# A table that fixes the order of every engine's queue in a fused attention and FFN kernel

## The chip, the cores and the metric

The kernel runs on one core of a Trainium2 chip. The metric is the device time of one execution in microseconds (us), the median of several. The core has TensorE (PE, matrix products and transposes), VectorE (DVE), ScalarE (ACT), GpSimd (POOL) and SyncE (SP, which here only issues transfers). Each takes its instructions in the order of its own queue.

## The reference

Attention over 8 batches, 8 heads, 576 positions and 64 dimensions, in two versions that are added: one over q, k and v averaged over groups of four positions and then repeated four times, one local, in which a position sees only those less than four away. The sum is laid out as 4608 tokens of 512 and goes through a two-layer FFN.

```python
factor = 4; scale = 1.0 / np.sqrt(D)
q_d = q.reshape(B, H, Sd, factor, D).mean(axis=3)      # k_d, v_d in the same way
out_up = np.repeat(sm_attn(q_d, k_d, v_d), factor, axis=2)
mask = np.abs(pos[:, None] - pos[None, :]) < factor
scores = np.where(mask, scale * np.matmul(q, k.transpose(0, 1, 3, 2)), -1000000000.0)
attn_out = out_up + np.matmul(softmax(scores), v)
x = attn_out.transpose(0, 2, 1, 3).reshape(B * S, H * D)      # 4608 x 512
h = x @ w_in                                                   # 512 x 2048
g = np.maximum(h, 0.0) + alpha * np.minimum(h, 0.0)
out = g @ w_out                                                # 2048 x 512
```

## The kernel before

Products run in fp32r with each operand split into a high and a low part (xh and xl, wih and wil, woh and wol, gh and gl), three products for one. The FFN is cut into 18 chunks of 256 tokens and each chunk into 8 steps of 256 hidden columns, 144 steps in all. Step number st does this:

- `hidden` (L784): 24 matmuls of 128x256 on TensorE into the PSUM tile h (two buffers, h0, h1, ...);
- `slopes` (L799, L801, L803): ScalarE makes t and sh, or scales h, from alpha;
- `larger` (L811 on DVE, or L76, a helper for additions on POOL): joins the two into t. POOL does it in 30 of the first 32 steps, DVE later;
- `split`: ScalarE casts t to gh (L816), POOL takes gl = t - gh (L73);
- `product` (L845): 12 matmuls of 128x512 into the chunk's two output tiles, o0_0 and o0_1 for chunk 0. After 8 steps ScalarE copies them to sg (L851) and SP stores them.

The weights come as 64-bit numbers and are decoded in the kernel by `make`, in 8 blocks for each matrix (raw0_0 to raw0_7 for w_in, raw1_0 to raw1_7 for w_out; the last ones in halves such as raw1_60 and raw1_61): ScalarE's magnitude (L197), DVE's L201, L202, L206 and L207, ScalarE's cast of the high part (L212 for wih, L216 for woh), DVE's low part (L220 for wil, L224 for wol).

The first batch of the attention is done by `first_batch`, four head pairs one after another (names with f: fs scores, fp and fpt probabilities, fpv their product with v, fxs, rest). Its last DVE lines are L534 (the sum of local and averaged attention, fxs) and L541 (xl = fxs - xh). Since x spans all heads, the first step can end its sums only with the fourth pair's xl0.

Later batches are done beside the FFN. `down` does the averaged attention of one batch and one head pair (qkT2_2 is batch 2, pair 2): loads ld (L247, three buffers), POOL's sums over four positions (L76, ld folded, then s2q, s2k, s2v), TensorE's transposes qkT (L265), ScalarE's copies qd and kd (L270, L273), scores s (L278), probabilities dp, their transposes pT (L302), ScalarE's copy th (L306), and pv (L312). `local` does the local attention in units on DVE, with some sums on POOL, and TensorE's transposes xp (L682) give the x tiles. qkT, s, pT, pv and xp share one PSUM tag of two buffers.

The order of the work is set in two ways. All these pieces stand in a list of events with planned times. Events before the time LISTED = 14 are handed to the tile scheduler, which orders each engine's queue by its own estimates, with some hints: `tc.issue_after` holds a load behind the load of a weight block (the table BEHIND), the first late magnitude behind a slope, and one local product behind the end of another unit. Events from 14 on are kept in the order of the list by `tc.manual_schedule()`. The last lines of the function are these (L1002 to L1011):

```python
    for t, _, f, args in events:
        if t < LISTED:
            f(*args)
    with tc.manual_schedule():
        for t, _, f, args in events:
            if t >= LISTED:
                f(*args)
```

Of the kernel before, what the change touches and what calls it, by code (L numbers as in the profile page):

```python
# [47 lines left out]
BEHIND = {(1, 0): ((0, 2), (0, 2)), (1, 1): ((1, 4), (0, 5)), (1, 2): ((1, 5), (1, 5))}  # L48
FAR = {3: 2, 4: 2, 5: 2, 6: 2}
LISTED = 14  # L50
JOINS = (0.04, 0.06)


@with_exitstack
def tile_attention_moe(ctx: ExitStack, tc: tile.TileContext, q, k, v, w_in, w_out, alpha, out):
# [24 lines left out]

# [43 lines left out]

# [7 lines left out]

    raws, turns, issued, sloped = {}, [0, 0], {}, {}
    weights_temp = []

    def load_raw(which, fp, blocks=(0, 1)):
        raw = raws.setdefault((which, fp), {})
        if fp < NP - 2:
            raw[None] = one.tile([128, 1024, 2], I32, tag=f"slot{turns[0] % 3}", name=f"raw{which}_{fp}")
# [2 lines left out]
        src = (w_in, w_out)[which].bitcast(I32)  # L150
        for c in blocks:
            if fp < NP - 2:
                dst = raw[None][:, 512 * c:512 * c + 512]
            elif fp == NP - 2:
                dst = raw[c] = late.tile([128, 512, 2], I32, tag="prod", name=f"raw{which}_{fp}{c}", bufs=PB)
            else:
                dst = raw[c] = late.tile([128, 512, 2], I32, tag=f"x{'hl'[c]}", name=f"raw{which}_{fp}{c}")
            if which == 0:
                issued[which, fp] = nc.sync.dma_start(dst.rearrange("p (k a) b -> p k (a b)", k=2),
                                  bass.AP(src.tensor, 256 * c * 2 * DF + 512 * fp, [[2 * DF, 128], [256 * DF, 2], [1, 512]]))  # L160
            else:
                row = 256 * fp + 128 * c
                issued[which, fp] = nc.sync.dma_start(dst.rearrange("p a b -> p (a b)"), src[row:row + 128, :])
# [8 lines left out]

    def make(which, fp, c=None):
# [12 lines left out]
        def magnitude():  # L188
# [7 lines left out]
            with tc.issue_after(sloped[0].ins) if (which, fp) == (0, N_EARLY) else nullcontext():  # L196
                nc.scalar.activation(f32(st["t"]), f32(st["raw"][:, :, :, 1]), AF.Abs)  # L197
# [31 lines left out]

# [137 lines left out]

# [8 lines left out]

# [6 lines left out]

# [202 lines left out]


    def local(u, t0, t1):
# [183 lines left out]

# [45 lines left out]

# [37 lines left out]

# [15 lines left out]


# [103 lines left out]

# [59 lines left out]
```

## Time and profile before

| | |
|---|---|
| median of 3 runs | 983.32 us (983.08 to 987.91) |
| profiled execution | 982.8 us |
| its span in the trace | 981.0 us |
| mean granted TensorE clock | 0.976 of full speed |
| busy: PE, DVE, ACT, POOL | 942.9, 819.5, 555.3, 527.6 us |

The profile is of one execution. Its span runs from the first to the last instruction; the execution's own time is 1.8 us longer. Busy time is the time in which an engine has an instruction in work; idle time of an engine is put down in the trace to what released it (in square brackets behind an instruction: how long the engine stood idle before it, and which instruction of which engine ended that). A full granted clock of TensorE is 2.4 GHz, half of it 1.2 GHz. Line numbers are those of the kernel before.

### The profile page before, as it was taken

What the parts mean: (1) busy time and instruction counts of PE and PEld (TensorE: products, weight loads), DVE (VectorE), ACT (ScalarE), POOL (GpSimd) and SP (SyncE); (2) the same over time, 40 slices, a digit from 0 to 9 for tenths busy, and PEclk for the clock granted to TensorE, in tenths of its full rate; (3) what the DMA queues carried; (4) which work ended last, traced back from release to release, by engine and by line L of the source; (5) the groups of instructions that cost most, each with busy time, mean ns of one, the idle gap of its engine ahead of it and who ended that gap; (6) DMA issues with size and microseconds to landing.
All of it is one profiled execution on the core that took longest, in us unless ns stands there. A gap on an engine that the chain in (4) does not pass through costs nothing.

```text
span 981.0 us, 17943 instructions
## 1 busy us (share of the span) xinstructions
PE 942.9 (96%) x6402; PEld 842.0 (86%) x6402; DVE 819.5 (84%) x1318; ACT 555.3 (57%) x1483; POOL 527.6 (54%) x642
## 2 busy tenths in 40 slices
PE   5878999999999999999999999999999999999998
PEld 4757887987888888989988899898899989999997
DVE  7999978888879999998889899899898889997111
ACT  4767776544645655556554655565556664544442
POOL 2055877787887546555537365555466633323221
PEclk9956999999999999999999999999999999999999
DMA  8946723132333322422322423332333321310000
GB/s 200 232 146 208 254 90 107 61 114 85 111 101 116 114 76 88 139 80 83 119 78 86 127 86 93 108 98 68 105 112 103 110 63 46 97 34 22 1 22 22
DMA packets 63197, 98.28 MB, mean 100 GB/s; under 512 B 23556, under 2 KB 28932, under 8 KB 63108
## 3 DMA queue, kind: packets, MB, share of 16 engines
q1 hardware_dynamic: 62916, 96.88, 32.8%
q8 instruction: 50, 0.82, 0.3%
q10 hardware_dynamic: 192, 0.26, 0.1%
q14 instruction: 39, 0.32, 0.1%
HBM read 87.67 MB, written 9.44 MB: 99 GB/s over the span
## 4 chain that ended last, share of the span: by engine, by line
PE 59%; DVE 11%; POOL 4%; ACT 3%; issue 2%; DMA 1%; SPq 0%; DVEq 0%; POOLq 0%
PE o L845 28%; PE h L784 27%; DVE lb L673 3%; DVE pv L670 2%; DVE qk L614 1%; PE s L278 1%; PE pv L312 1%; DVE t L811 1%; DVE ls L618 1%; PE xp L682 1%; POOL t L76 1%; PE pT L302 1%; DVE xf L698 1%; ACT t L799 1%; POOL gl L73 1%
## 5 line engine op out<-in xcount | busy, mean ns | idle before, releaser
L73 POOL TENSOR_TENSOR gl<-t,gh 128x512 fp32r<-128x512 f32 x144 | 186.3, 1294 | 323.4 <-ACT gh L816 303.3
L799 ACT ACTIVATE t<-h,slope 128x256 f32<-128x256 f32 x288 | 136.3, 473 | 128.8 <-PE h L784 105.7
L845 PE MATMUL o<-woh,gh 128*128 128x512 f32 x576 | 192.8, 405 | 2.5 <-ACT gh L816 1.1
L784 PE MATMUL h<-xh,wih 128*128 128x256 f32 x1152 | 188.0, 285 | 2.6 <-ACT sh L801 1.9
L845 PE MATMUL o<-wol,gh 128*128 128x512 f32 x576 | 185.7, 393 | 0.0
L845 PE MATMUL o<-woh,gl 128*128 128x512 f32 x576 | 185.4, 393 | 0.0
L784 PE MATMUL h<-xh,wil 128*128 128x256 f32 x1152 | 180.7, 279 | 0.0
L784 PE MATMUL h<-xl,wih 128*128 128x256 f32 x1152 | 180.5, 279 | 0.0
L784 PEld LDWEIGHTS h<-xh,wih 128*128 128x128 f32 x1152 | 162.8, 190 | 13.0 <-ACT sh L801 2.6
L816 ACT CAST gh<-t 128x512 fp32r<-128x512 f32 x144 | 89.5, 622 | 140.3 <-DVE t L811 81.6
L76 POOL TENSOR_TENSOR ld<-ld 72x256 f32<-72x256 f32 x168 | 131.9, 787 | 67.4 <-DMA ld<-in_q 64.8
L784 PEld LDWEIGHTS h<-xh,wil 128*128 128x128 f32 x1152 | 155.3, 190 | 0.3
L784 PEld LDWEIGHTS h<-xl,wih 128*128 128x128 f32 x1152 | 154.6, 190 | 0.1
L811 DVE TENSOR_TENSOR t<-h,t 128x512 f32<-128x512 f32 x114 | 78.3, 687 | 88.2 <-ACT h L803 87.8
L618 DVE TENSOR_REDUCE ls<-qk 128x12 f32<-128x768 f32 (+1 forms) x126 | 136.2, 1083 | 3.1
L845 PEld LDWEIGHTS o<-woh,gl 128*128 128x128 f32 x576 | 108.0, 188 | 24.0
L845 PEld LDWEIGHTS o<-wol,gh 128*128 128x128 f32 x576 | 108.0, 188 | 23.1 <-DVE temp L207 0.2
L673 DVE TENSOR_TENSOR lb<-lb,pv 128x384 f32<-128x384 f32 x202 | 114.0, 564 | 5.9
L845 PEld LDWEIGHTS o<-woh,gh 128*128 128x128 f32 x576 | 99.1, 188 | 18.9 <-issue 2.6
L803 ACT ACTIVATE h<-h,sign 128x256 f32<-128x256 f32 x228 | 100.2, 439 | 0.0
L670 DVE TENSOR_TENSOR pv<-v,lb 128x1152 f32<-128x1152 f32 x84 | 93.6, 1115 | 2.7
L614 DVE TENSOR_TENSOR qk<-k,qp 128x768 f32<-128x768 f32 (+1 forms) x78 | 84.0, 1078 | 4.6 <-ACT qp L607 4.6
(151 smaller groups left out, 1185.7 us busy)
## 6 DMA issues: line engine op xcount, KB each, us to landing
k<-in_k SPq DMA_DIRECT2D x41, 384.0 KB
v<-in_v SPq DMA_DIRECT2D x41, 384.0 KB
out<-sg SPq DMA_DIRECT2D x140, 64.0 KB
raw<-in_moe_w_in SPq DMA_DIRECT2D x16, 512.0 KB
raw<-in_moe_w_out SPq DMA_DIRECT2D x16, 512.0 KB
ld<-in_q SPq DMA_DIRECT2D x56, 144.0 KB
ld<-in_k SPq DMA_DIRECT2D x56, 144.0 KB
ld<-in_v SPq DMA_DIRECT2D x56, 144.0 KB
```

The source lines that it names most:

```text
L73: nc.gpsimd.tensor_tensor(o, a, b, op=ALU.subtract)
L76: nc.gpsimd.tensor_tensor(o, a, b, op=ALU.add)
L614: nc.vector.tensor_tensor(st["pr"][:, :nd], window(tiles[u, "k"], half, d0, nd), st["qp", half].unsqueeze(1).to_broadcast([128, nd, 2, 192 ...
L618: nc.vector.tensor_reduce(out=st["s"][:, half, d0:d0 + nd, :].rearrange("p a b -> p (a b)"), in_=st["pr"][:, :nd].rearrange("p a h (t d) - ...
L670: nc.vector.tensor_tensor(st["pr"][:, :nd], window4(tiles[u, "v"], half, d0, nd), prob(half, d0, nd), op=ALU.mult)
L673: nc.vector.tensor_tensor(st["acc"], st["acc"], st["pr"][:, i], op=ALU.add)
L784: nc.tensor.matmul(ph[:, j], w[:, m, 128 * o:128 * o + 128], x[:, m, :], start=(i == 0), stop=(i == 11))
L799: nc.scalar.activation(t[:, j], hs[st][:, j], AF.Copy, scale=slope[:, f:f + 1])
L803: nc.scalar.activation(other[:, j], hs[st][:, j], AF.Copy, scale=sign[:, f:f + 1])
L811: nc.vector.tensor_tensor(gs[st], hs.pop(st), gs[st], op=ALU.max)
L816: nc.scalar.copy(gh, t)
L845: nc.tensor.matmul(outs[c][m], g[:, j, 128 * m:128 * m + 128], wo[w][n][:, o, :], start=(f == 0 and i == 0), stop=(f == NF - 1 and i == 2))
```

## The change

A table ORDERS holds for each of PE, DVE, Activation, Pool and SP the names of the tiles in the order in which they are to be written; `h1*8` is eight operations on tile h1, `temp@1` the second of the operations on temp that are still open. After all operations have been emitted, a loop goes through the instructions, looks up the next one of each named tile, and ties each operation of an engine behind the one ahead of it on the same engine. `manual_schedule`, BEHIND, the calls of `issue_after` and what they needed go. The numbers of instructions stay.

```diff
-BEHIND = {(1, 0): ((0, 2), (0, 2)), (1, 1): ((1, 4), (0, 5)), (1, 2): ((1, 5), (1, 5))}
+ORDERS = {
+    "PE": """
...
+    o2_0 o2_1 o2_0 o2_1 o2_0 o2_1 o2_0 o2_1 o2_0 o2_1 pT2_1_0*3 pT2_1_1*3 h23*24 qkT2_2*4 xp5_0*3 o2_0 o2_1 o2_0
...
-            with tc.issue_after(sloped[0].ins) if (which, fp) == (0, N_EARLY) else nullcontext():
-                nc.scalar.activation(f32(st["t"]), f32(st["raw"][:, :, :, 1]), AF.Abs)
+            nc.scalar.activation(f32(st["t"]), f32(st["raw"][:, :, :, 1]), AF.Abs)
...
-            behind = BEHIND.get((b, hp))
-            with tc.issue_after(issued[behind[i // 3]].ins) if behind else nullcontext():
-                nc.sync.dma_start(st[i].rearrange("p g f d -> p (g f d)"),
-                                  bass.AP(src.tensor, (b * H + 2 * hp + i % 2) * HEAD, [[512, 72], [1, 512]]))
+            nc.sync.dma_start(st[i].rearrange("p g f d -> p (g f d)"),
+                              bass.AP(src.tensor, (b * H + 2 * hp + i % 2) * HEAD, [[512, 72], [1, 512]]))
...
-            with tc.issue_after(ended[3].ins) if (u, half, d0) == (4, 0, 0) else nullcontext():
-                nc.vector.tensor_tensor(st["pr"][:, :nd], window(tiles[u, "k"], half, d0, nd),
-                                        st["qp", half].unsqueeze(1).to_broadcast([128, nd, 2, 192]), op=ALU.mult)
+            nc.vector.tensor_tensor(st["pr"][:, :nd], window(tiles[u, "k"], half, d0, nd),
+                                    st["qp", half].unsqueeze(1).to_broadcast([128, nd, 2, 192]), op=ALU.mult)
...
-    with tc.manual_schedule():
-        for t, _, f, args in events:
-            if t >= LISTED:
-                f(*args)
+    for t, _, f, args in events:
+        if t >= LISTED:
+            f(*args)
+
+    queues = {e: [] for e in ORDERS}
+    for i in nc.cur_bb.bb.instructions:
+        e = str(i.engine).split(".")[-1]
+        ap = getattr(i.outs[0], "bass_ap", None) if len(i.outs) else None
+        if e in ORDERS and ap is not None:
+            queues[e].append((re.sub(r"_\d+$", "", ap.tensor.name), i))
+    for e, listed in ORDERS.items():
+        by_name, line = {}, []
+        for name, i in queues[e]:
+            by_name.setdefault(name, []).append(i)
+        for name, _, n in (x.partition("*") for x in listed.split()):
+            name, _, k = name.partition("@")
+            line += [by_name[name].pop(int(k or 0)) for _ in range(int(n or 1))]
+        placed = {i.name for i in line}
+        line += [i for _, i in queues[e] if i.name not in placed]
+        for i, j in zip(line, line[1:]):
+            tc.add_manual_dep(j, i.name, mybir.DependencyInfo(mybir.DependencyClass.NoSync, mybir.DependencyReason.DATA),
+                              reason="order")
```

What moves, engine by engine: SP's queue is the same before and after. PE's differs in its first 445 us or so, DVE's, ACT's and POOL's about as far; behind that all queues are as they were. Three places follow, before and then after. The line numbers behind the change are those of the changed program (L534, L571 and L1045 there are L265, L302 and L784 before; L363 and L360 are L76 and L73; L807, L800, L493, L474, L475, L479 and L480 are L541, L534, L220, L201, L202, L206 and L207).

The first place is DVE, where the first batch's fourth head pair meets the decode of the fourth weight blocks. DVE before:

```order
L202 TENSOR_SCALAR temp_208<-temp_208 128x1024
L220 TENSOR_TENSOR wil1_855<-temp_208,wih1_854 128x4x256
L534 TENSOR_TENSOR fxs30_796<-fpv30_787,fod3_785 128x256
L206 SCALAR_TENSOR_TENSOR temp_208<-raw1_3_882,temp_208 128x1024
L282 TENSOR_REDUCE dnb1_0_1082<-s1_0_1067 96x3
L534 TENSOR_TENSOR rest_106<-fpv38_813,fod3_785 128x64
L201 TENSOR_SCALAR temp_208<-temp_208 128x1024
L541 TENSOR_TENSOR xl0_108<-fxs30_796,xh0_107 128x256
```

DVE with the change:

```order
L800 TENSOR_TENSOR fxs30_796<-fpv30_787,fod3_785 128x256
L480 SCALAR_TENSOR_TENSOR temp_208<-raw0_3_872,temp_208 128x1024
L474 TENSOR_SCALAR temp_208<-temp_208 128x1024
L475 TENSOR_SCALAR temp_208<-temp_208 128x1024
L807 TENSOR_TENSOR xl0_108<-fxs30_796,xh0_107 128x256
L493 TENSOR_TENSOR wil1_855<-temp_208,wih1_854 128x4x256
L479 SCALAR_TENSOR_TENSOR temp_208<-raw1_3_882,temp_208 128x1024
L800 TENSOR_TENSOR rest_106<-fpv38_813,fod3_785 128x64
L480 SCALAR_TENSOR_TENSOR temp_208<-raw1_3_882,temp_208 128x1024
L474 TENSOR_SCALAR temp_208<-temp_208 128x1024
L800 TENSOR_TENSOR fxs34_809<-fpv34_800,fod3_785 128x256
L551 TENSOR_REDUCE dnb1_0_1082<-s1_0_1067 96x3
```

fxs30 went ahead of the last decode operations of block raw0_3, and xl0 ahead of wil1, of raw1_3's first operations, of rest and of dnb1_0.

The second place is PE near step 23, where qkT2_2 is the transpose for batch 2, pair 2, and o2_0 and o2_1 belong to chunk 2. PE before:

```order
L845 MATMUL o2_0_2492<-wol2_915,gh20_2704 128x512
L845 MATMUL o2_1_2493<-wol2_915,gh20_2704 128x512
L845 MATMUL o2_0_2492<-woh2_914,gl20_2705 128x512
L845 MATMUL o2_1_2493<-woh2_914,gl20_2705 128x512
L265 MATMUL qkT2_2_2877<-ident_75,s2q2_2_2609 128x72 x2
L265 MATMUL qkT2_2_2877<-ident_75,s2k2_2_2691 128x72 x2
L784 MATMUL h23_2884<-xh2_1758,wih3_1283 128x256 x4
L784 MATMUL h23_2884<-xh2_1758,wil3_1284 128x256 x4
L784 MATMUL h23_2884<-xl2_1759,wih3_1283 128x256 x4
```

PE with the change:

```order
L1105 MATMUL o2_0_2490<-woh2_914,gl20_2703 128x512
L1105 MATMUL o2_1_2491<-woh2_914,gl20_2703 128x512
L571 MATMUL pT2_1_0_2834<-ident_75,dp2_1_2693 72x96 x3
L571 MATMUL pT2_1_1_2838<-ident_75,dp2_1_2693 72x96 x3
L1045 MATMUL h23_2882<-xh2_1758,wih3_1283 128x256 x4
L1045 MATMUL h23_2882<-xh2_1758,wil3_1284 128x256 x4
L1045 MATMUL h23_2882<-xl2_1759,wih3_1283 128x256 x4
L1045 MATMUL h23_2882<-xh2_1758,wih3_1283 128x256 x4
L1045 MATMUL h23_2882<-xh2_1758,wil3_1284 128x256 x4
L1045 MATMUL h23_2882<-xl2_1759,wih3_1283 128x256 x4
L534 MATMUL qkT2_2_2875<-ident_75,s2q2_2_2607 128x72 x2
L534 MATMUL qkT2_2_2875<-ident_75,s2k2_2_2689 128x72 x2
```

Before, the twelve o matmuls of step 20 stood between pT2_1_1 and qkT2_2 (the last four are shown), and h23 behind qkT2_2; now the twelve stand ahead of pT2_1_0, and all 24 matmuls of h23 stand between pT2_1_1 and qkT2_2.

The third place is POOL in the second batch's second head pair (ld1_1_4 and ld1_1_5 are its tiles of v, s2v1_1 their sums; t3 belongs to step 3). POOL before:

```order
L76 TENSOR_TENSOR ld1_1_4_1157<-ld1_1_4_1157 72x2x128
L76 TENSOR_TENSOR s2k1_1_1194<-ld1_1_3_1125 72x2x64
L76 TENSOR_TENSOR ld1_1_5_1201<-ld1_1_5_1201 72x2x128
L76 TENSOR_TENSOR t0_1019<-sh0_1020,t0_1019 128x512
L76 TENSOR_TENSOR s2v1_1_1248<-ld1_1_4_1157 72x2x64
L76 TENSOR_TENSOR s2v1_1_1248<-ld1_1_5_1201 72x2x64
L73 TENSOR_TENSOR gl0_1033<-t0_1019,gh0_1032 128x512
L76 TENSOR_TENSOR t1_1073<-sh1_1074,t1_1073 128x512
```

POOL with the change:

```order
L363 TENSOR_TENSOR t1_1073<-sh1_1074,t1_1073 128x512
L360 TENSOR_TENSOR gl1_1087<-t1_1073,gh1_1086 128x512
L363 TENSOR_TENSOR t2_1133<-sh2_1134,t2_1133 128x512
L363 TENSOR_TENSOR ld1_1_5_1201<-ld1_1_5_1201 72x2x128
L360 TENSOR_TENSOR gl2_1163<-t2_1133,gh2_1162 128x512
L363 TENSOR_TENSOR t3_1218<-sh3_1219,t3_1218 128x512
L363 TENSOR_TENSOR ld1_1_4_1157<-ld1_1_4_1157 72x2x128
L363 TENSOR_TENSOR s2v1_1_1248<-ld1_1_4_1157 72x2x64
L363 TENSOR_TENSOR s2v1_1_1248<-ld1_1_5_1201 72x2x64
```

The sums of v for that pair went from between t0 and gl0 to behind t3.

## Rows read from the trace of the kernel before

**Rows 1.** The page, busy time of each engine: us, share of the span, instructions.

```profile
PE 942.9 (96%) x6402; PEld 842.0 (86%) x6402; DVE 819.5 (84%) x1318; ACT 555.3 (57%) x1483; POOL 527.6 (54%) x642
```

**Rows 2.** Stretches: us, busy PE, PEld, DVE, ACT, POOL, then PEclk, DMA share, GB/s.

```profile
50.00:75.00 25.00, 19.27 (x122) 14.80 (x122) 24.97 (x43) 15.66 (x41) 13.05 (x12) 0.50 0.38 135
75.00:100.00 25.00, 20.14 (x139) 17.38 (x138) 24.63 (x31) 18.11 (x43) 15.26 (x12) 0.68 0.70 232
100.00:125.00 25.00, 25.00 (x161) 22.35 (x160) 22.82 (x30) 18.34 (x48) 22.09 (x26) 1.00 0.69 232
225.00:250.00 25.00, 22.70 (x143) 19.89 (x142) 21.66 (x42) 11.12 (x35) 19.79 (x26) 0.93 0.26 80
330.00:900.00 570.00, 569.05 (x3894) 513.07 (x3893) 521.56 (x841) 319.62 (x867) 296.64 (x368) 1.00 0.29 89
```

**Rows 3.** Timeline of DVE, 80 to 100 us: start us, us, engine, line, operation.

```profile
80.70 1.22 DVE L220 TENSOR_TENSOR wil<-temp,wih 128x1024 fp32r<-128x1024 f32 x1
...
81.83 0.42 DVE L534 TENSOR_TENSOR fxs<-fpv,fod 128x256 f32<-128x256 f32 x1
...
84.55 0.41 DVE L541 TENSOR_TENSOR xl<-fxs,xh 128x256 fp32r<-128x256 f32 x1
...
99.66 4.40 DVE L220 TENSOR_TENSOR wil<-temp,wih 128x1024 fp32r<-128x1024 f32 x1
```

**Rows 4.** Waits of DVE in 0 to 130 us: total us, times, longest.

```profile
DVE fv L493 <- DMA fv<-in_v: 3.9, 2, 2.1
```

**Rows 5.** Timeline of PE, 50 to 160 us, as rows 3, idle time before in brackets.

```profile
72.23 2.13 PE L515 MATMUL fpt<-ident,fp 128*70 128x128 f32 x9 [3.22 <-DVE fp L510]
...
92.69 0.73 PE L784 MATMUL h<-xh,wih 128*128 128x256 f32 x4 [1.87 <-ACT sh L801]
...
99.36 0.51 PE L845 MATMUL o<-woh,gh 128*128 128x512 f32 x1 [1.05 <-ACT gh L816]
...
126.79 0.51 PE L784 MATMUL h<-xh,wih 128*128 128x256 f32 x2 [0.70 <-ACT wih L212]
...
149.13 0.74 PE L845 MATMUL o<-woh,gh 128*128 128x512 f32 x2 [0.67 <-ACT woh L216]
...
157.71 0.51 PE L845 MATMUL o<-woh,gh 128*128 128x512 f32 x1 [0.73 <-ACT sg L851]
```

**Rows 6.** Timeline of PE, 225 to 330 us, the three longest idle times.

```profile
231.03 0.50 PE L265 MATMUL qkT<-ident,s2q 72*128 72x72 f32 x2 [2.24 <-ACT th L306]
...
259.75 0.34 PE L265 MATMUL qkT<-ident,s2q 72*128 72x72 f32 x2 [1.42 <-ACT th L306]
...
289.72 0.65 PE L682 MATMUL xp<-ident,x 128*128 128x128 f32 x4 [0.93 <-ACT kd L273]
```

**Rows 7.** The chain of waits, 226 to 265 us: start us, us, what.

```profile
227.19 1.28 POOL t L76
...
230.66 0.32 ACT th L306
...
231.77 3.97 PE h L784 x24
...
248.75 2.07 DMA ld<-in_v
...
260.22 2.79 PE h L784 x24
```

**Rows 8.** Timeline of POOL, 98 to 114 us, as rows 3.

```profile
98.62 1.85 POOL L76 TENSOR_TENSOR s2v<-ld 72x128 f32<-72x128 f32 x2
...
113.21 1.32 POOL L76 TENSOR_TENSOR t<-sh,t 128x512 f32<-128x512 f32 x1
```

**Rows 9.** Timeline of SP, the transfers' queue, 80 to 160 us, as rows 3.

```profile
118.16 0.90 SPq L163 DMA_DIRECT2D raw<-in_moe_w_out  x2
...
124.09 1.68 SPq L163 DMA_DIRECT2D raw<-in_moe_w_out  x2
```

**Rows 10.** Timeline of ACT, 135 to 144 us, as rows 3.

```profile
135.18 0.66 ACT L197 ACTIVATE temp<-raw 128x512 f32<-128x512 f32 x1
```

More of the change, by code (lines that the diff above doesn't have):

```diff
@@ L1 @@
+import re
 import struct
-from contextlib import ExitStack, nullcontext
+from contextlib import ExitStack
 import concourse.bass as bass
@@ L132, in load_alpha @@
         nc.vector.tensor_tensor(gain, sign, slope, op=ALU.subtract)
-    raws, turns, issued, sloped = {}, [0, 0], {}, {}
+    raws, turns = {}, [0, 0]
     weights_temp = []
@@ L158, in load_raw @@
             if which == 0:
-                issued[which, fp] = nc.sync.dma_start(dst.rearrange("p (k a) b -> p k (a b)", k=2),
+                nc.sync.dma_start(dst.rearrange("p (k a) b -> p k (a b)", k=2),
                                   bass.AP(src.tensor, 256 * c * 2 * DF + 512 * fp, [[2 * DF, 128], [256 * DF, 2], [1, 512]]))
@@ L162, in load_raw @@
                 row = 256 * fp + 128 * c
-                issued[which, fp] = nc.sync.dma_start(dst.rearrange("p a b -> p (a b)"), src[row:row + 128, :])
+                nc.sync.dma_start(dst.rearrange("p a b -> p (a b)"), src[row:row + 128, :])
     def weight_tiles(which, n):
@@ L544, in first_batch @@
         return load_pair, load_windows, pair
-    tiles, ended = {}, {}
+    tiles = {}
     def unit_base(u):
@@ L675, in last @@
         def last(half):
-            ended[u] = nc.vector.tensor_tensor(st["x"][:, 3 * half:3 * half + 3].rearrange("p t h d -> p h t d"), st["acc"], st["far", half], op=ALU.add)
+            nc.vector.tensor_tensor(st["x"][:, 3 * half:3 * half + 3].rearrange("p t h d -> p h t d"), st["acc"], st["far", half], op=ALU.add)
         def flip(i):
@@ L800, in slopes @@
             if st in EARLY:
-                sloped[st] = nc.scalar.activation(other[:, j], hs[st][:, j], AF.Relu, scale=gain[:, f:f + 1])
+                nc.scalar.activation(other[:, j], hs[st][:, j], AF.Relu, scale=gain[:, f:f + 1])
             else:
```

284 lines of the change are left out of this document (added).

## The prediction

> **What bounds the kernel now.** I read the page's busy shares first, then the busy time by stretches, then TensorE's timeline for every place where it stood idle, and only then the other engines at those places. TensorE (PE) is busy 942.9 of 981.0 us, VectorE (DVE) 819.5 [rows 1]. The stretches tell two different kernels [rows 2]. From 100 us on TensorE is full: 25.00 of 25 us between 100 and 125, 569.05 of 570 between 330 and 900. So what a later stage can give is only its few idle places. Before 100 us it is not full: 19.27 of 25 between 50 and 75 and 20.14 between 75 and 100, and at a granted clock of 0.50 and 0.68, while DVE is busy 24.97 and 24.63 of the same 25. There the end is set by DVE's queue, which holds the first attention batch and the decode of the weights.
>
> After 330 us there is nothing to win in TensorE's queue, and the change leaves the order from about 450 us on as it was. What is won or lost before 330 us therefore goes through to the end one for one, if weights and x tiles keep up. The sum is made against the profiled execution, 982.8 us; the median of the three runs, 983.32, lies 0.5 above it.
>
> **The change, part by part.** It adds and removes no instruction on any compute engine and no transfer: the same operations stand in other places. The tie from each operation to the one ahead on its own engine costs nothing in itself, because an engine takes its queue in order anyway; what it removes is 18 to 47 semaphore waits per engine, hidden in the same queues, and the program's hints that held some loads and activations behind others. SyncE's queue, which issues the transfers, keeps its order. I put all this at nothing, bounds 0 to 1 us in the whole; what covers it is each queue's own backlog.
>
> *The start (before about 90 us).* The first chunk of the FFN needs xl0 of the fourth head pair, DVE's L541 at 84.55 [rows 3]. Before, five instructions stand ahead of it that are not ahead of it now: L220 at 80.70, then L206, the L282 reduce, L534 of the rest and L201. From the row at 80.70 to that at 84.55 is 3.85 us; fxs30, 0.34 us from start to start, still stands ahead, so 3.51 us are gone from in front of the instruction that lets TensorE start the steps in earnest, and nothing new comes ahead of it. DVE has no idle time there that would have absorbed it [rows 2]. I take **3.5 us**. Upper bound 5.5: the two waits for in_v, 3.9 us in sum [rows 4], now have ten and more other instructions ahead of them, and I let them give half, 2 us. Lower bound 0: TensorE still waits 3.22 us for DVE's fp before it [rows 5], which has its own causes, and the decode of the later weights is due next.
>
> *92 to 100 us.* TensorE waits 1.87 us for ScalarE's sh and 1.05 for gh [rows 5]. In the new order pT of the second batch's first pair is 6.5 us of TensorE work later and four more steps are rearranged around them. But the first gh has to go through h, slopes, POOL's add and the cast whatever stands where, so one such wait stays. Between 0 and 2.9 us (1.87 + 1.05); I take **0.5**, nearest to the wait that must stay.
>
> *126 to 158 us.* Three waits, 0.70 for wih, 0.67 for woh and 0.73 for sg [rows 5]: 2.10. Two are for decoded weights. In the new order the decode of w_out's third block goes 12.5 us of DVE work later and parts of the fourth block 3 us earlier, nearer to the order of use. I take **1.0**; bounds -2 (a new wait on a late block) and 2.1.
>
> *231 to 330 us.* Three waits stand out: 2.24, 1.42 and 0.93 [rows 6], 4.6 us in all. After the first the h group of 24 matmuls took 3.97 us, against 2.79 for the same group at 260 us [rows 7]: 1.2 more. The granted clock is 0.93 on the mean of that stretch [rows 2], so it was at its lower level, 1.2 GHz, for a part of it, right behind the idle time. That makes 5.8. The first place is plain. qkT2_2 needs a PSUM bank that ScalarE frees by copying th, and the chain shows th at 230.66 behind gh, t, h, t, h, and all of these behind POOL's t of 227.19 [rows 7]. TensorE stands at the head of its queue with qkT2_2 while h23, which needs none of this, waits behind it. Now h23's 24 matmuls go first. They cover 2.75 us, more than the 2.24 it stood idle. The same cure is at 259.75: twelve o matmuls now stand between the two pT of that pair, so the bank of the first is free before qkT needs it. The wait for kd I expect to stay, since the x tiles come from DVE as before. I take **4.9**: 2.24 + 1.2 + 1.42; bounds 0 and 5.8.
>
> Sum 3.5 + 0.5 + 1.0 + 4.9 = 9.9; 982.8 - 9.9 = 972.9, and 0.5 for the median: **973.4 us**. The bounds of the terms taken together are a loss of 2 and a gain of 16.3 us, but they don't fall together: an earlier TensorE asks earlier for weights and x.
>
> **The rivals.**
>
> *A, the weights take the start back.* From 100 us DVE decodes while POOL adds, and then its instructions are longer: L220 took 4.40 us at 99.66 against 1.22 at 80.70 [rows 3]. If TensorE comes 3.5 us sooner, the h4 and h6 steps wait for blocks that are no sooner. Then terms one to three vanish and only the last is left: 982.8 - 4.9 + 0.5 = 978.4. For it: the wih and woh waits exist now. Against it: the halves of wil2 move 5 us forward in DVE's queue. The Trainium skill, "SBUF — State Buffer", section "Who interferes with whom", says that DVE and GpSimd share one port pair as an exclusive lock and that issue order decides who blocks; by it a new order can lengthen or shorten each of these instructions, and one such meeting more on the path, at 4.40 - 1.22 = 3.2 us, would make my forecast about 976.6. The row at 99.66 fits the rule but does not show which of the two blocked.
>
> *B, the stalls only change places.* ScalarE still waits for POOL's t before it can copy th, two PSUM banks still serve five kinds of tile, and a tile that waits for a bank later could stop TensorE just as long. The start's 3.5 us would then be spent by new stalls too: 982 to 983.5, no change. Against it: at 231 and 259 us independent work of the right length was put in front.
>
> *C, all of it goes.* The sum of the upper bounds, 5.5 + 2.9 + 2.1 + 5.8 = 16.3: 982.8 - 16.3 + 0.5 = 967.0. For it: the new order was moved at every place where TensorE waits. Against it: the first gh's chain stays.
>
> *D, slower: the last blocks of w_out come late.* POOL's fold of the fifth ld tile of the second pair and the two s2v folds behind it now stand behind the add t3. Before, the s2v folds were done at 100.47 (98.62 + 1.85) and t3 ran at 113.21 [rows 8]. The next ld transfers reuse the folds' buffers, and SyncE's queue, in which they stand, is in order: the blocks raw1_60 at 118.16 and raw1_70 at 124.09 [rows 9] stand behind them and behind later folds that follow t5 and gl6 now. I estimate 8 to 9 us later from the places of these adds on POOL's timeline, so near 127 and 132. ScalarE first reads raw1_60 at 135.18 [rows 10], and has this read eight places earlier now, with the slopes of h7 and h8 behind it. If a block is not there, ScalarE stops, both h banks stay full and TensorE stops with them. A small transfer took 2.07 us to land [rows 7], so it would fit with little slack. It decides against the change once each of the two blocks keeps ScalarE some 5 us and with it the steps to 230 us: 982.8 + 10 for the waits, less 3.5 for the start, plus 1.2 for one more fall of the clock, plus 0.5 for the median: 991.0.
>
> *E, the table moves nothing that matters*, since the scheduler's own order was near it: then 983.3, which B's chance holds.
>
> **How the numbers follow.** A run of this kernel can tell about 0.5%, 4.9 us, from no change, so "faster" ends at 978.4 and "slower" begins at 988.2. Forecast (969 to 977) 0.42; A (976.5 to 980.5) 0.20, half of it under 978.4; B and E (980.5 to 984) 0.15; C (964 to 969) 0.13; D (988.2 to 993) 0.10. Faster 0.42 + 0.10 + 0.13 = 0.65; same 0.10 + 0.15 = 0.25; slower 0.10. The range leaves out D and about half of C: 966 to 984. Within it the forecast's own 969 to 977 is likeliest.
>
> **What would show each step.** Right: xl0 of the fourth pair ends near 81 instead of 85 us, and the granted clock reaches 1.00 some 3 us sooner; no idle row ahead of qkT2_2 and its h23 group near 2.75 us; fewer than 3 us of idle between 225 and 330; the last stretch the same but some 10 us sooner. Wrong: DVE idle for ScalarE's decode before 100 us (the start was not DVE's order); a wait of TensorE for wih, wil or woh of over 2 us between 95 and 160 (A); ScalarE idle before the first read of raw1_60 or raw1_70 (D); pT, s or qkT with new idle of 1 to 2 us (B).

## The result, and the profile after

The changed kernel takes **972.27 us** (median, 971.34 to 973.06), the kernel before 983.68 beside it: a ratio of 0.9875, 95% interval 0.9845 to 0.9904, so 11.4 us faster. The forecast was 973.4 and its range 966 to 984. The sum came out nearly right. Its terms did not, and most of what follows is about that.

The profiled execution took 971.34 us (span 969.5, mean granted clock 0.982). The page's busy times of the changed kernel, to be held against [rows 1]:

```profile
PE 942.5 (97%) x6402; PEld 845.4 (87%) x6402; DVE 811.0 (84%) x1318; ACT 555.7 (57%) x1483; POOL 525.5 (54%) x642
```

The counts are the same and TensorE's busy time is within 0.4 us. What went is idle time of TensorE: 38.1 us of the span before, 27.0 now. VectorE was busy 8.5 us less with the same 1318 instructions. The same stretches as in [rows 2], changed kernel, same columns:

```profile
50.00:75.00 25.00, 18.75 (x119) 15.03 (x115) 25.00 (x43) 16.68 (x46) 12.51 (x11) 0.54 0.41 143
75.00:100.00 25.00, 21.62 (x158) 19.78 (x155) 23.71 (x34) 18.87 (x44) 12.08 (x11) 0.77 0.54 178
100.00:125.00 25.00, 24.74 (x161) 21.34 (x160) 23.92 (x33) 20.36 (x53) 20.86 (x21) 1.00 0.63 221
...
225.00:250.00 25.00, 24.19 (x176) 21.95 (x176) 22.90 (x37) 14.63 (x42) 20.21 (x25) 1.00 0.43 132
...
330.00:900.00 570.00, 568.98 (x3888) 513.42 (x3888) 510.91 (x828) 318.41 (x858) 295.15 (x365) 1.00 0.29 89
```

From 330 to 900 us TensorE is as full as before. Between 225 and 250 TensorE does 176 matmuls instead of 143, at a clock of 1.00 instead of 0.93. These are the idle places that TensorE's timeline of the changed kernel shows between 85 and 460 us (the bracket is the idle time before the instruction and what ended it):

```profile
89.86 1.22 PE L1045 MATMUL h<-xh,wih 128*128 128x256 f32 x4 [2.68 <-ACT sh L1062]
...
95.09 0.74 PE L1045 MATMUL h<-xh,wih 128*128 128x256 f32 x4 [0.70 <-ACT sh L1062]
...
102.98 0.39 PE L1045 MATMUL h<-xh,wil 128*128 128x256 f32 x1 [0.26 <-DVE wil L493]
...
134.13 0.73 PE L1105 MATMUL o<-wol,gh 128*128 128x512 f32 x2 [0.77 <-DVE wol L497]
...
231.90 0.74 PE L1045 MATMUL h<-xh,wih 128*128 128x256 f32 x4 [0.81 <-ACT xh L974]
```

The three waits of [rows 6] are gone, and three smaller ones of the kernel before with them (0.33 at 255.10, 0.29 at 284.75, 0.57 at 328.21). The first wait of the FFN is longer than in that one trace of the kernel before: 2.68 us against 1.87 in [rows 5]. The four matmuls behind it took 1.22 us, because the granted clock was at its half level, 1.2 GHz, there. Neither is the mark of the new order. In the kernel before the first four behind the wait took 0.73, but 1.5 us later four like them were slow too:

```profile
94.17 1.02 PE L784 MATMUL h<-xh,wih 128*128 128x256 f32 x4
```

And the four other traces of the old order (e1, e2, e5 and e10, described below) have waits of 1.78 to 2.96 us at this place. The longest is in e10:

```profile
90.52 1.22 PE L1043 MATMUL h<-xh,wih 128*128 128x256 f32 x4 [2.96 <-ACT sh L1060]
```

**How leads are read from here on.** A step's end says little where other work has moved across it. So I add up TensorE's matmuls in each trace, each at what its shape takes at full clock, and note how much sooner than the profiled execution of the kernel before (positive) a trace reaches the same sum of work. The columns are the place in the trace of before; the last two are differences.

| us sooner at | 90 | 120 | 180 | 220 | 450 | 120 to 180 | 220 to 450 |
|---|---|---|---|---|---|---|---|
| changed kernel | 3.1 | 1.5 | 3.4 | 3.4 | 11.4 | 2.0 | 8.1 |
| *old order to 180 us* | | | | | | | |
| e1_before_table | -1.1 | -1.7 | -1.8 | -1.8 | -0.5 | -0.1 | 1.3 |
| e2_late_only | -0.5 | -0.4 | -0.5 | -6.6 | 1.8 | 0.0 | 8.3 |
| e5_h23_first | 0.4 | -0.3 | -0.2 | -0.2 | 1.7 | 0.1 | 1.9 |
| e10_folds_ahead | 3.2 | 2.1 | 1.9 | 2.1 | 5.3 | -0.2 | 3.2 |
| *new order to 90 us, in part with an edit* | | | | | | | |
| e3_early_only | 3.6 | 1.7 | 3.4 | 3.7 | 7.7 | 1.7 | 4.0 |
| e4_qkt_back | 3.3 | 0.5 | 2.4 | 2.3 | 9.5 | 1.9 | 7.2 |
| e7_xl1_late | 2.7 | -1.0 | 2.5 | 2.5 | 10.7 | 3.5 | 8.2 |
| e7b_xl0_late | -2.8 | -1.4 | 0.8 | 0.8 | 9.1 | 2.2 | 8.3 |
| e8m_folds | 3.2 | -2.2 | 1.1 | 1.0 | 9.3 | 3.3 | 8.3 |
| e9_start | 2.3 | -1.4 | 1.5 | 1.5 | 9.6 | 2.9 | 8.2 |
| e9m_start_folds | 3.4 | -0.5 | 2.2 | 2.2 | 10.6 | 2.7 | 8.4 |
| e11_pool_mid_back | 1.5 | -0.9 | -1.4 | -13.4 | -5.1 | -0.5 | 8.3 |

Each row is one execution. The rows of the old order differ among themselves by 4.3 us at 90 us and still by 3.7 at 180, so a lead of 3 us at the start cannot be read from one pair of traces. The two difference columns are steadier: in the column 120 to 180 the old order stays within 0.3 us, and in the last column the traces with the late part of the new table lie at 8.1 to 8.4, all but e4.

### The profile page after: what moved, and what is told of

Same layout as the page of the kernel before. It is cut to its first block, busy times and chain, and to the rows that moved or that the text cites. A ratio compares the mean times of both kernels' runs of the same rounds, so it can differ in the third digit from the quotient of the medians.

```text
span 969.5 us, 17939 instructions
## 1 busy us (share of the span) xinstructions
PE 942.5 (97%) x6402; PEld 845.4 (87%) x6402; DVE 811.0 (84%) x1318; ACT 555.7 (57%) x1483; POOL 525.5 (54%) x642
## 4 chain that ended last, share of the span: by engine, by line
PE 71%; DVE 12%; issue 2%; ACT 1%; POOL 1%; DMA 1%; DVEq 0%; SPq 0%; ACTq 0%; POOLq 0%
PE o L1105 33%; PE h L1045 32%; DVE lb L935 3%; DVE pv L932 2%; PE s L547 2%; DVE qk L876 2%; PE pv L581 2%; DVE t L1072 1%; DVE ls L880 1%; PE xp L944 1%; PE pT L571 1%; DVE xf L960 1%; DMA raw<-in_moe_w_out 1%; PE qkT L534 1%; ACT t L1060 1%
## 5 line engine op out<-in xcount | busy, mean ns | idle before, releaser
L360 POOL TENSOR_TENSOR gl<-t,gh 128x512 fp32r<-128x512 f32 x144 | 187.2, 1300 | 303.1 <-ACT gh L1077 296.4
L1045 PE MATMUL h<-xh,wih 128*128 128x256 f32 x1152 | 187.8, 285 | 4.2 <-ACT sh L1062 3.4
L1045 PE MATMUL h<-xh,wil 128*128 128x256 f32 x1152 | 180.2, 278 | 0.3 <-DVE wil L493 0.3
L1045 PE MATMUL h<-xl,wih 128*128 128x256 f32 x1152 | 180.4, 279 | 0.0
L1045 PEld LDWEIGHTS h<-xh,wih 128*128 128x128 f32 x1152 | 162.3, 190 | 13.5 <-ACT sh L1062 4.1
L363 POOL TENSOR_TENSOR ld<-ld 72x256 f32<-72x256 f32 x168 | 126.8, 758 | 75.5 <-DMA ld<-in_k 47.2
L1045 PEld LDWEIGHTS h<-xh,wil 128*128 128x128 f32 x1152 | 154.4, 189 | 0.7 <-DVE wil L493 0.7
L1045 PEld LDWEIGHTS h<-xl,wih 128*128 128x128 f32 x1152 | 153.8, 189 | 0.5 <-issue 0.4
```

The lines of the kernel that those rows point to most:

```text
L360: nc.gpsimd.tensor_tensor(o, a, b, op=ALU.subtract)
L363: nc.gpsimd.tensor_tensor(o, a, b, op=ALU.add)
L1045: nc.tensor.matmul(ph[:, j], w[:, m, 128 * o:128 * o + 128], x[:, m, :], start=(i == 0), stop=(i == 11))
```

## The experiments

All kernels but the changed one are the changed kernel with other tables. "Early" and "late" are the parts of the table ahead of and behind a cut at about 195 us, where both orders have issued the same set of operations on each engine. Ratios are to the kernel before on the same chip.

| run | median us | before us | ratio | 95% |
|---|---|---|---|---|
| e1_before_table | 984.38 | 983.52 | 1.0016 | 0.9992 to 1.0040 |
| e2_late_only | 983.85 | 983.52 | 0.9993 | 0.9968 to 1.0018 |
| e3_early_only | 975.34 | 983.52 | 0.9920 | 0.9893 to 0.9948 |
| e4_qkt_back | 973.54 | 983.52 | 0.9903 | 0.9868 to 0.9938 |
| e5_h23_first | 982.62 | 983.39 | 0.9989 | 0.9966 to 1.0012 |
| e10_folds_ahead | 979.81 | 983.39 | 0.9969 | 0.9946 to 0.9991 |
| e7_xl1_late | 972.51 | 983.39 | 0.9892 | 0.9871 to 0.9913 |
| e7b_xl0_late | 972.56 | 983.39 | 0.9893 | 0.9861 to 0.9925 |
| e8m_folds | 972.78 | 983.01 | 0.9876 | 0.9838 to 0.9914 |
| e9_start | 973.24 | 983.01 | 0.9884 | 0.9847 to 0.9921 |
| e9m_start_folds | 971.82 | 983.01 | 0.9868 | 0.9831 to 0.9904 |
| e11_pool_mid_back | 987.21 | 983.01 | 1.0026 | 1.0004 to 1.0047 |

### The ties alone, and the two halves

**e1_before_table**: the table lists the old order on all engines, so only the ties are new and the hints gone.

```diff
 ORDERS = {
-    the new order
+    the order of the kernel before
```

> The changed program with a table that holds the order of the kernel before on every engine: the ties alone, without the moves. Theory (the moves carry everything, the ties and the dropped hints nothing): 982 to 985 us, no change. Rival (the ties, fewer semaphore waits, or the dropped hints speed the queues up): 980 us or less.

The ratio is 1.0016, its interval holds 1 (from 0.8 us faster to 3.9 slower). Ties and dropped hints bring no gain, so the order brings the 11.4 us. The prediction said that the ties remove semaphore waits. They don't: the trace of e1 has as many as the kernel before on every engine, and only the new order has fewer. The run gives something else too. TensorE's idle place ahead of qkT2_2 is there, but not the fall of the clock behind it:

```profile
225.00:250.00 25.00, 22.71 (x156) 19.88 (x155) 22.27 (x44) 12.90 (x40) 21.17 (x28) 1.00 0.25 78
```

The clock is 1.00 where [rows 2] have 0.93, with the same order and the same idle time. In the lead table that is the 1.3 us which this run gains between 220 and 450. So 1.3 of every number in that column belongs to the one profiled execution of before.

**e2_late_only** and **e3_early_only**: one half of the table new, the other old.

```diff
-    new order, early and late
+    e2: old order early, new order late
+    e3: new order early, old order late
```

> Order of before up to step 18 or so (about 195 us) on every engine, the new order behind it. Theory (the two parts add up; the lead of the new order was 3.4 us at 220 us and 10.8 at 330): 983.7 - 7.5 to 8 = about 976. Rival (the late gain needs the early one, since x tiles and weights come by absolute time): 979 or more.

> The new order up to about 195 us, that of before behind it. Theory (the parts add up): 983.7 - 3.4 = about 980.3, with the waits at 231 to 330 us back, 5.8 us in sum. Rival (the early lead is spent again at the old stalls): 982 or more.

The halves don't add up: neither time is the one that the theory gave, 976 for e2 and 980.3 for e3. The early half alone gains 8.2 us, the late half alone nothing (983.85), both together 11.4. In e2 the late half does gain its 8.3 us from 220 on, but the joint costs 6 us just ahead of that. TensorE's timeline and the stretch 213 to 219 us of e2 (columns as in [rows 2]):

```profile
214.78 1.23 PE L1043 MATMUL h<-xh,wih 128*128 128x256 f32 x4 [3.48 <-ACT sh L1060]
```

```profile
213.00:219.00 6.00, 4.22 (x25) 4.22 (x26) 5.83 (x8) 2.19 (x6) 5.92 (x8) 0.72 0.05 17
```

POOL is busy 5.92 of 6 us while TensorE stands. ScalarE's sh stands behind a cast gh, and that gh waited for POOL's t:

```profile
213.01 0.62 ACT L1075 CAST gh<-t 128x512 fp32r<-128x512 f32 x1 [4.76 <-POOL t L361]
```

Ahead of that t POOL's row has sums of ld and local products pv: the late order counts on sums that the old early order hasn't done. In e3 TensorE's queue around qkT2_2 is the old one, with h23 behind it, and yet the idle place there is all but gone, while those further on are back. Timeline of TensorE, e3, its first three idle places from 200 us on:

```profile
224.70 0.35 PE L529 MATMUL qkT<-ident,s2q 72*128 72x72 f32 x2 [0.16 <-ACT th L570]
...
247.32 0.41 PE L566 MATMUL pT<-ident,dp 96*72 96x96 f32 x3 [0.41 <-DVE xf L955]
...
251.98 0.35 PE L529 MATMUL qkT<-ident,s2q 72*128 72x72 f32 x2 [1.42 <-ACT th L570]
```

2.24 us at 231 in before, 0.16 here. What cured that wait lies ahead of 195 us.

### The wait at 231 us: TensorE's order or POOL's

**e5_h23_first** moves only TensorE's piece at step 23 (the second place shown with the change) into the old order; **e4_qkt_back** takes only that piece back in the new one.

```diff
-pT2_1_0*3 pT2_1_1*3 (o2_0 o2_1)*6 qkT2_2*4 h23*24
+(o2_0 o2_1)*6 pT2_1_0*3 pT2_1_1*3 h23*24 qkT2_2*4
```

That is e5, e4 is the reverse.

> The order of before on every engine, only TensorE's piece at step 23 as in the new table: the twelve o matmuls, pT, h23, then qkT2_2. Theory 1 (the prediction's: the place of qkT2_2 is the wait): 2.24 us of idle and 1.2 of clock gone and not given back, 983.5 - 3.4 = about 980. Theory 2 (POOL's backlog at 197 to 230 us is the wait, with t18 to t21 late; the stall only moves to the next use of its results): 982.5 to 984, with new idle of TensorE between 231 and 245 us.

> The new order, only TensorE's piece at step 23 as before: pT of batch 2, pair 1, the twelve o matmuls, qkT2_2, then h23. Theory (TensorE's own order hid the wait for the bank): idle of 1.5 to 2.2 us ahead of qkT2_2 is back, and 1.2 us for the clock if it falls: 974 to 976 us. Rival (ScalarE's order alone brings th forward: it now comes 0.8 us behind pT, where it came 4.6 us behind): no idle ahead of qkT2_2, 972.3 us.

**e10_folds_ahead** leaves TensorE's order as before and moves twelve of POOL's sums over four positions (batch 2, pair 1) about one step ahead in its queue:

```diff
-gl14 t15 gl15 xl2 xl2 ld2_1_0 s2q2_1 ld2_1_1 s2q2_1 t16 gl16 ld2_1_2 s2k2_1 ld2_1_3 s2k2_1
-t17 gl17 ld2_1_4 s2v2_1 ld2_1_5 s2v2_1 pv6_4_0
+gl14 ld2_1_0 s2q2_1 ld2_1_1 s2q2_1 t15 gl15 xl2 xl2 ld2_1_2 s2k2_1 ld2_1_3 s2k2_1 t16 gl16
+ld2_1_4 s2v2_1 ld2_1_5 s2v2_1 t17 gl17 pv6_4_0
```

> The order of before on every engine, only POOL's twelve sums of batch 2's second head pair one step earlier (ahead of t15, t16 and t17, where POOL stood idle up to 2.9 us). Theory 2 (POOL's backlog is the wait at 231 us): t18 to t21 some 2.5 us earlier against TensorE, the idle of 2.24 us ahead of qkT2_2 and the clock's 1.2 gone: 979.5 to 981. Theory 1 (TensorE's place of qkT2_2): the idle stays, 983.5.

e5's median is 0.8 us below before, not to be told from nothing. TensorE's timeline of e5 shows where the wait went:

```profile
232.68 0.52 PE L942 MATMUL xp<-ident,x 128*128 128x128 f32 x3 [1.05 <-ACT kd L540]
...
249.27 0.52 PE L942 MATMUL xp<-ident,x 128*128 128x128 f32 x3 [0.54 <-DVE drs L560]
...
253.31 0.41 PE L569 MATMUL pT<-ident,dp 96*72 96x96 f32 x3 [0.53 <-DVE xf L958]
...
257.97 0.35 PE L532 MATMUL qkT<-ident,s2q 72*128 72x72 f32 x2 [1.42 <-ACT th L573]
```

h23 does cover the wait for th, but what comes behind qkT2_2 is now late: 1.05 us, then 0.54 that was not there before. The trace puts the 1.05 down to kd, which ended at 232.54. VectorE's x, which these transposes read, ended at 232.53, and it had waited for POOL's product pv. So the wait moved, in part at least, to the next result that POOL was late with. e10, with TensorE's order untouched, gains 3.6 us by the medians and 1.9 (3.2 less 1.3) by the lead table. The medians alone don't tell e10 from e5, since their intervals overlap; the traces do. TensorE's idle places between 200 and 345 us come to 5.8 us in e1, 5.3 in e5 and 4.3 in e10. POOL's timelines tell why. First e1, the old order (the rows are t15 with the idle time ahead of it, t17, the sum of the sixth ld tile, t18 and t21):

```profile
185.09 1.30 POOL L361 TENSOR_TENSOR t<-sh,t 128x512 f32<-128x512 f32 x1 [2.88 <-ACT sh L1060]
...
200.81 1.29 POOL L361 TENSOR_TENSOR t<-sh,t 128x512 f32<-128x512 f32 x1
...
205.86 0.74 POOL L361 TENSOR_TENSOR ld<-ld 72x256 f32<-72x256 f32 x1
...
209.77 1.30 POOL L361 TENSOR_TENSOR t<-sh,t 128x512 f32<-128x512 f32 x1
...
228.93 1.31 POOL L361 TENSOR_TENSOR t<-sh,t 128x512 f32<-128x512 f32 x1
```

and e10 (the sum, t17, t18, t21):

```profile
195.88 0.74 POOL L361 TENSOR_TENSOR ld<-ld 72x256 f32<-72x256 f32 x1
...
197.12 1.30 POOL L361 TENSOR_TENSOR t<-sh,t 128x512 f32<-128x512 f32 x1
...
203.63 1.29 POOL L361 TENSOR_TENSOR t<-sh,t 128x512 f32<-128x512 f32 x1
...
222.96 1.30 POOL L361 TENSOR_TENSOR t<-sh,t 128x512 f32<-128x512 f32 x1
```

In the old order POOL stands idle 2.88 us at 182, and from 197 to 237 it is busy 36.15 of 40 us: sums of ld, local products pv, the adds t and the low parts gl in one row, so t18 to t21 are each late. In e10 the sum is 10 us and t18 6.1 us earlier, while the whole run is 3.7 us earlier there (lead 1.9 against -1.8): 2.4 us of backlog are gone. ScalarE's wait for t18 shrinks with it, from 5.67 us (gh at 211.11 in e1) to 3.19 (204.95 in e10). TensorE's wait ahead of qkT2_2 shrinks by 1.53, from e1

```profile
232.81 0.34 PE L532 MATMUL qkT<-ident,s2q 72*128 72x72 f32 x2 [2.23 <-ACT th L573]
```

to e10

```profile
226.84 0.34 PE L532 MATMUL qkT<-ident,s2q 72*128 72x72 f32 x2 [0.70 <-ACT th L573]
```

e4, the changed kernel with TensorE's old piece, keeps nearly all of the gain: 0.9903 against 0.9875 with intervals that overlap, a lead 220 to 450 of 7.2 instead of 8.1, and 0.35 us of idle time ahead of qkT2_2. Its time, 973.54, lies between what the theory and the rival gave, and the idle of 1.5 to 2.2 us that the theory wanted back is not there. So the place of h23 is worth 1 us at most in the new order (not told from none by the medians) and next to nothing in the old. The wait at 231 us was POOL's backlog: with POOL's sums done sooner it falls from 2.23 to 0.70 (e10), and with the whole early half to 0.16 (e3), while TensorE's piece stays as it was.

**e11_pool_mid_back** is the test from the other side: the new table, with POOL's order between about 155 and 200 us alone taken back (the end of the edit is shown).

```diff
...
-gl14 s2k2_1 xl2@1 xl2 t15 gl15 ld2_1_4 t16 ld2_1_3 ld2_1_5 gl16 t17 s2k2_1 s2v2_1 pv6_4_0
-pv5_4_0 gl17 pv6_4_0 s2v2_1 t18
+gl14 t15 gl15 xl2 xl2 ld2_1_0 s2q2_1 ld2_1_1 s2q2_1 t16 gl16 ld2_1_2 s2k2_1 ld2_1_3 s2k2_1
+t17 gl17 ld2_1_4 s2v2_1 ld2_1_5 s2v2_1 pv6_4_0 pv5_4_0 pv6_4_0 t18
```

> The new table, only POOL's order between about 155 and 200 us as before, so the sums of batch 2's second pair are late again. Theory 2 (POOL's backlog carries the gain at 231 us): TensorE idle again between 205 and 245 us, 3 us or more with the clock, 975 to 977. Theory 1 (TensorE's and ScalarE's new places cover it): 972.3 to 973.

987.21 us, 15 us above the changed kernel and far past both expectations. TensorE's timeline, the four largest of its idle places between 150 and 226 us:

```profile
162.14 0.74 PE L1100 MATMUL o<-woh,gl 128*128 128x512 f32 x2 [1.14 <-POOL gl L355]
...
186.22 0.55 PE L939 MATMUL xp<-ident,x 128*128 128x128 f32 x3 [2.74 <-DVE x L933]
...
196.99 0.72 PE L1040 MATMUL h<-xl,wih 128*128 128x256 f32 x4 [1.48 <-POOL xl L355]
...
221.61 1.22 PE L1040 MATMUL h<-xh,wih 128*128 128x256 f32 x4 [3.49 <-ACT sh L1057]
```

They make 8.9 us, and behind the 2.74 and the 3.49 the clock falls (0.76 on the mean of 185 to 192 us, 0.72 of 220 to 226). From 220 on the run gains the same 8.3 us as the others. POOL's queue is in order, and the new orders of the other engines don't fit POOL's old one. The run doesn't say that POOL's new order alone would gain those 15 us: it is a mismatch as in e2, with the same wait of 4.76 us of ScalarE's gh for POOL's t (219.84).

### The start

**e7_xl1_late** and **e7b_xl0_late** put the fourth head pair's xl1 or xl0 some 2.5 and 5.5 us of VectorE work later in the new table; **e9_start** moves xl1 with its xh1 and the first slopes forward.

```diff
 e7, DVE
-xl1 wol1 wol1 temp
+wol1 wol1 temp xl1
 e7b, DVE
-xl0 wil1 temp rest temp temp
+wil1 temp rest temp temp xl0
 e9, DVE
-xl0 wil1 temp rest temp temp fxs34 dnb1_0 temp xl1
+xl0 fxs34 xl1 wil1 temp rest temp temp dnb1_0 temp
 e9, Activation
-wih1 temp woh1*2 xh1 t0 sh0 t0 sh0
+wih1 xh1 temp t0 sh0 t0 sh0 woh1*2
```

> The new table, only DVE's last xl1 of the first batch behind the two wol1 and one more decode instruction, 2.6 us later. If the start's gate is xl1 (sh0 lies in the memory that xl1's input frees, and h2 waits for sh0): h2 begins 2.6 us later, 972.3 + 2.6 = about 975, or less where the decode then gives some back. If it is xl0, as predicted: 972.3.

> The new table, only DVE's xl0 of the first batch's fourth pair behind the five instructions that stood ahead of it before, 3.5 us later. If xl0 is the gate, as predicted: h0 and all behind it 3.5 us later, about 975.8. If xl1 and sh0 are: h0 ends some 3.5 us later but h2 waits for sh0 anyway, so 0.5 to 1.5 us: 972.8 to 973.8.

> The new table, only DVE's last fxs and xl1 of the first batch straight behind xl0, ScalarE's xh1 ahead of a decode step and the slopes of h0 ahead of the two woh1. TensorE's 2.68 us ahead of h2 and most of the low clock behind it should go, h2 begins near 87.5 instead of 89.9. If the transfer of raw1_60 is the gate behind it: no gain in the end, 972 to 972.6, and ScalarE waits for it longer than 2.4 us. If not: 969 to 970.5.

The three end at 972.51, 972.56 and 973.24: nothing that can be told from 972.27. e7's time is the one expected if xl0 is the gate, e7b's the one if it is not, so neither sets the end. In the changed kernel VectorE's rows of the fourth pair are xl0 and xl1, and then the wil that [rows 3] have at 4.40 us:

```profile
82.23 0.42 DVE L807 TENSOR_TENSOR xl<-fxs,xh 128x256 fp32r<-128x256 f32 x1
...
88.15 0.41 DVE L807 TENSOR_TENSOR xl<-fxs,xh 128x256 fp32r<-128x256 f32 x1
...
100.62 2.31 DVE L493 TENSOR_TENSOR wil<-temp,wih 128x1024 fp32r<-128x1024 f32 x1
```

xl0 is 2.3 us earlier than the row of before. Over all traces it begins at 82.38 to 86.21 in the old order and at 81.93 to 83.74 in the new one (87.78 in e7b, which holds it back). But ScalarE's sh of the first step then waits for xl1 (the profile's timeline of ScalarE has sh at 88.60 behind "DVE xl"), and h2 waits for that sh. e7 shows the link: xl1 later, and h2 begins at 92.37 behind an idle time of 4.77 instead of 2.68. In e9 h2 begins 0.9 us earlier, behind 1.00, and the time is lost at the next step. TensorE and ScalarE in e9:

```profile
88.97 0.74 PE L1040 MATMUL h<-xh,wih 128*128 128x256 f32 x4 [1.00 <-ACT sh L1057]
...
96.44 0.79 PE L1040 MATMUL h<-xh,wih 128*128 128x256 f32 x4 [4.46 <-ACT sh L1057]
```

```profile
92.50 0.64 ACT L465 ACTIVATE temp<-raw 128x512 f32<-128x512 f32 x1 [0.79 <-DMA raw<-in_moe_w_in]
...
94.12 0.63 ACT L465 ACTIVATE temp<-raw 128x512 f32<-128x512 f32 x1 [0.59 <-DMA raw<-in_moe_w_in]
```

The next sh stands in ScalarE's queue behind reads of w_in blocks that have not landed. Coming sooner meant waiting for weights there. At 120 us of the lead table no lead is left that stands out of the spread: from -2.2 to 1.7 in the new order, from -1.7 to 2.1 in the old.

**e8m_folds** moves POOL's sums of batch 1, pairs 1 and 2, forward again in the new table, so that w_out's late blocks are issued sooner; **e9m_start_folds** does this and e9's edit.

```diff
-ld1_1_5 gl2 t3 ld1_1_4 s2v1_1*2 ld1_2_0 t4 gl3 s2q1_2 gl4 t5 ld1_2_2 ld1_2_1 ld1_2_3
+ld1_1_5 ld1_1_4 s2v1_1*2 gl2 t3 ld1_2_0 s2q1_2 t4 gl3 ld1_2_1 ld1_2_2 gl4 s2q1_2 s2k1_2 ld1_2_3 t5
...
```

> The new table, only POOL's sums of batch 1's second and third pair moved forward again, into places where POOL stood idle. In the new kernel ScalarE waited 2.44 us for raw1_60, which went out at 124.6 instead of 118.2. Theory (these late folds hold SyncE's queue and eat the start's gain, the small form of the slow rival): raw1_60 goes out some 5 us earlier, no wait of ScalarE for it, TensorE's 0.77 us at 134 gone: 970 to 971.5 us. Rival (the decode on DVE is the gate there, not the transfer): 972.3, DVE waits or is full in its place.

> Both edits together. If the transfer is what eats an earlier start: the gains add, 968 to 970 us. If the decode on DVE is the gate: 971 to 972.3.

972.78 and 971.82, both the changed kernel's time within what can be measured. In the changed kernel SyncE issues raw1_60 and raw1_70 at these times (the transfers' queue, to be held against [rows 9]), and ScalarE waits for the first:

```profile
124.63 0.83 SPq L439 DMA_DIRECT2D raw<-in_moe_w_out  x2
...
131.23 0.83 SPq L439 DMA_DIRECT2D raw<-in_moe_w_out  x2
```

```profile
131.34 0.63 ACT L470 ACTIVATE temp<-raw 128x512 f32<-128x512 f32 x1 [2.44 <-DMA raw<-in_moe_w_out]
```

In e8m the two blocks went out later, not sooner, at 125.89 and 134.03. ScalarE's wait and TensorE's 0.77 us at 134 are gone all the same, but TensorE waits 1.52 us for wil at 105 in their place (0.26 in the changed kernel), and 4.21 ahead of h2. So this run doesn't settle what sooner blocks are worth. No kernel of these beats the changed one by more than the measurement's own uncertainty; e9m's 971.82 is the lowest median.

## Why the prediction was right, and where its steps failed

**The frame held.** After 330 us TensorE's row didn't change, and the ties brought and cost nothing that can be told (e1). VectorE filled the stretch from 50 to 75 us and still does: 25.00 of 25.

**The start, 3.5 us: made, and lost again.** In this pair of traces TensorE is 3.1 us ahead at 90 us, close to the number. That alone says little, since two runs of the old order differ there by 4.3 (e1, e10). But those two are 4.0 apart at 60 us already. Counted in the same way from 75 to 90 us alone, the eight traces with xl0 at its new place gain 2.7 to 5.1 us, the four other traces of the old order -0.2 to 1.1, and e7b, which holds xl0 back, loses 1.3: TensorE stands there 2.42 us for xl at 88.25. So xl0 does let TensorE start sooner, as predicted. By the lead table the eight lose 1.6 to 5.4 us again between 90 and 120 us, the old order 1.1 at most. Delaying xl0 or xl1 costs nothing at the end, and moving them forward gives nothing. The step that failed is the sentence that what is won before 330 us "goes through to the end one for one, if weights and x tiles keep up". The sh that waits for xl1 was overlooked as the next gate (2.68 us in the changed kernel, 4.77 in e7), and where it comes sooner, in e9, ScalarE waits for blocks of w_in.

**92 to 100 us, 0.5 forecast.** A loss of 1.6 (lead 3.1 to 1.5 at 120), outside its bounds of 0 to 2.9, though e10 with the old order loses 1.1 there too. The one wait that "must stay" became 2.68, 0.70 and 0.26 us, against 1.87 and 1.05 in the one trace that was read. Rival A said that the start is taken back, and so it is; but its mark, a wait of TensorE of over 2 us for a weight block, did not come. In the changed kernel it is ScalarE's sh that holds TensorE up; late blocks show only in e9, where ScalarE waits 0.79 and 0.59 us for them, and in e8m, where TensorE waits 1.52 us for wil.

**126 to 158 us, 1.0 forecast: 2.0.** All three waits of [rows 5] there went, 2.10 us, and one of 0.77 came for wol. Every run of the new order to 180 us gains 1.7 to 3.5 between 120 and 180 (e11 has POOL's old order from 155 on), every run of the old order 0.1 at most. This, and the early part's share past 220 us below, is its lasting gain, and not the start.

**231 to 330 us, 4.9 forecast: 8.1, over the upper bound of 5.8.** The step that failed reads "The first place is plain": that qkT2_2 stands ahead of h23 was what the row showed, not why th was late. e5 shows that h23's new place alone buys no time that can be told from none. e10 and e3 show that the wait shrinks to 0.70 and 0.16 when POOL does most of the sums of batch 2, pair 1, earlier. The prediction had the chain in hand, th "behind gh, t, h, t, h, and all of these behind POOL's t of 227.19", and stopped one link short of asking why that t was late. Of the 8.1, 4.0 come with the early half of the table (e3); 1.3 of these are the low clock of one execution, and 2.7 are left. The other 4.1 come with the late half: the 1.42 that was forecast, the 0.93 for kd that I expected "to stay", and the 0.33, 0.29 and 0.57 that I left out. These make 3.5. Which of the late moves cured each of them was not tried one by one.

**The rivals.** B: one new wait past 200 us, 0.81 for xh. D: the late blocks came, issued at 124.6 and 131.2 (forecast 127 and 132), and ScalarE stood 2.44 us, but for one of the two only, and TensorE lost 0.77 us, not 10. C, everything gone, was not reached: TensorE still waits at the start, and the time is 5.3 us above C's.

So a start that was counted too high (4.0 for the first two terms, 1.5 found in this pair) and a late part counted too low (4.9, 8.1 found) met in a sum of 9.9 against 11.4. That the two errors cancelled was luck; the time was right in part for other reasons than those I gave.

What stays open: which moves carry the 2 us between 120 and 180 us, and which the 4.1 of the late half. An instruction of VectorE at 100 us is shorter in the new order (below), but no run isolates this.

## What to carry to other kernels

The row that stands idle names the last link: before an instruction is moved around a wait, follow the chain back to the in-order engine that has a backlog, and look for its idle time earlier on, where that work could have been done. An order table is one piece across all engines: half of it cost its whole gain at the joint (e2), and one engine's part taken back cost 15 us (e11), so test pieces both ways, each alone and each left out. A few us at the start of a kernel can't be read from one pair of traces; compare medians, or count the same short stretch in several runs, from just ahead of the place that was moved.

## What was not expected of the hardware

- The same order does not start the same: at 90 us of TensorE's work the old order's traces lie 4.3 us apart (e1, e10); 4.0 of it are there at 60 us, and 3.7 are left at 180 us.
- The same idle time of 2.2 us ahead of qkT2_2 was followed by a lower clock in one execution (0.93 on the mean of 225 to 250 us) and not in another of the same order (1.00, e1): the 1.2 us that I added for it were a matter of the one trace.
- The same VectorE instruction, wil of 128x1024, took 4.40 us before, 2.31 in the changed kernel at the same place of the program, and 1.22 where it stands at 80.70 in [rows 3]. It goes with the order and not with the execution: 4.40 to 4.42 in all five traces of the old order, 2.30 to 2.32 in all nine of the new one. Over the whole execution VectorE was busy 8.5 us less with the same 1318 instructions.
- POOL's rows beside that wil tell who was held up, which the prediction left open. First the kernel before (wil from 99.66 to 104.06), then the changed kernel (wil from 100.62 to 102.93):

```profile
100.44 1.28 POOL L73 TENSOR_TENSOR gl<-t,gh 128x512 fp32r<-128x512 f32 x1
101.69 1.29 POOL L76 TENSOR_TENSOR t<-sh,t 128x512 f32<-128x512 f32 x1
```

```profile
101.84 2.25 POOL L363 TENSOR_TENSOR t<-sh,t 128x512 f32<-128x512 f32 x1
```

Before, POOL's gl and t took their usual 1.3 us though both begin after wil, and wil ended 1.1 us behind them: VectorE was held up. In the changed kernel POOL's t took 1 us more than usual, so a part of the delay fell on POOL. What decides between the two is not shown.
